# Chunk transposes by DMA, bias in rows, a fixed sync queue and a new order of copies, in a fused attention and MLP kernel

## The chip, the cores and the metric

The kernel runs on one core of a Trainium2 chip. Times are device microseconds of one execution, as the median of several runs. A profile records one execution (of the kernel before a further one of 171.52 us); its span, from first to last instruction, is about 1.7 us shorter than the time. Engines: PE (matrix multiply), PEld (its weight loads), DVE (vector), ACT (activation functions), POOL, and SP, whose queue issues most DMA transfers. L228 is line 228 of that kernel's source; between the two kernels the lines shift by up to four.

## The reference

The input has 2048 rows of 448 columns in bf16. The rows are normalised, and two branches read them: an attention over a window of 8 keys at distance 2, with 16 heads of 28 columns, and an MLP with 1792 hidden columns. The output is the input plus the product of the branches.

```python
xn = _layernorm(x)
s = attention(xn, wqkv, wo)          # 16 heads, Dh = 28, W = 8, dilation 2
g = _silu(gelu(xn @ w1 + b1) @ w2 + b2)
return x + s * g
```

## The kernel before

The rows are cut into four chunks of 512. Feed-forward 1 of a chunk (hT, 14 tiles in seven pairs, k = 0 to 6) alternates with a phase of attention units: scores S, exponential and mask (E), weighted sum psO and its normalisation. Between the units stand feed-forward 2 (ps_y), v, and the output jobs (ps_s, sg, o_t). The order on PE, ACT, DVE and POOL is the program's own. These parts matter:

```python
psA = ctx.enter_context(tc.tile_pool(name="psA", bufs=2, space=PSUM))   # pairs of ps_h, S
psB = ctx.enter_context(tc.tile_pool(name="psB", bufs=4, space=PSUM))   # all else, and pairs 0 and 3 of ps_h
# ... loads on the sync queue: x chunk 0, wv, wraw, x chunk 1, then
nc.sync.dma_start(b1t[:], B_b1.rearrange("(m f) -> f m", f=P))          # 2-byte elements
# ... w1, w2, b2bc, x chunk 2, x chunk 3, 16 pieces of wo

def feed_forward_1(c, ps, wos):
    nc.scalar.preload_act_table_set(SET_GELU)
    for k in range(0, MT // 2, 2):
        ...                                    # pairs k and k+1 with their gelu
        if k == 2 and c in (1, 2):
            q_job(c + 1, 0); k_job(c + 1, 0, nc.vector.tensor_copy)
        if k in (2, 4) and c == 0:             # chunk 1 transposed on PE
            for j in (k - 2, k - 1):
                ln_put(nx + j, ln_tr(nx + j), nc.vector.tensor_copy)
        if c and k in (2, 4 if c == 3 else 6): # tanh on ACT, g on DVE
            ...                                # two silu_job
        for _ in range(2):
            if k >= (2 if c == 3 else 4) and wos:
                wo_job(wos.pop(0))
    nc.scalar.preload_act_table_set(SET_EXP)
    if c + 2 < NC:
        ln_rstd(nx + 4, 4)

# first unit of a phase: scores, exponentials and masks, then q and k of groups 2 and 3,
# then psO
```

The softmax here doesn't subtract the row's maximum and nothing guards it: scores larger than these inputs give would overflow.

Of the kernel before, what the change touches and what calls it, by code (L numbers as in the profile page):

```python
# [9 lines left out]
BF16 = mybir.dt.bfloat16  # L10
# [6 lines left out]
P = 128  # L17
# [16 lines left out]
def kernel(  # L34
# [46 lines left out]
    lnv = const.tile([P, NT], F32, name="lnv")  # L81
    ident = const.tile([P, P], BF16, name="ident")
    eps_t = const.tile([P, 1], F32, name="eps_t")
    b1t = const.tile([P, MT], BF16, name="b1t")
    b1f = const.tile([P, MT], F32, name="b1f")
    b2bc = const.tile([P, D], BF16, name="b2bc")
    mk_gen = const.tile([P, QW], BF16, name="mk_gen")
# [14 lines left out]
    for dst, c0, c1 in ((wv, 2 * D, 3 * D), (wraw, 0, 2 * D)):  # L102
        nc.sync.dma_start(dst[:, 0:3, 0:c1 - c0], A_wqkv[0:384, c0:c1].rearrange("(k p) f -> p k f", p=P))
        nc.sync.dma_start(dst[:64, 3, 0:c1 - c0], A_wqkv[384:448, c0:c1])
    nc.sync.dma_start(x_sb[1][:, :, :], dram_rows(x_par, 4, 4))
    nc.sync.dma_start(b1t[:], B_b1.rearrange("(m f) -> f m", f=P))
    for c0, c1 in ((0, F // 2), (F // 2, F)):
        nc.sync.dma_start(w1[:, 0:3, c0:c1], B_w1[0:384, c0:c1].rearrange("(k p) f -> p k f", p=P))  # L108
        for r in (0, 64):
            nc.sync.dma_start(w1[r:r + 64, 3, c0:c1], B_w1[384:448, c0:c1])  # L110
    nc.sync.dma_start(w2[:, :, :], B_w2.rearrange("(m p) c -> p m c", p=P))
    nc.sync.dma_start(b2bc[:], B_b2.rearrange("(o d) -> o d", o=1).to_broadcast((P, D)))  # L112
    nc.sync.dma_start(x_sb[2][:, :, :], dram_rows(x_par, 8, 4))
    nc.sync.dma_start(x_sb[3][:, :, :], dram_rows(x_par, 12, 4))


    nc.gpsimd.memset(ident[:], 0.0)
# [11 lines left out]
    for tl in (qT, kT):  # L129
        nc.vector.memset(tl[:, :, 0:LEAD].bitcast(U32), 0)  # L130
        nc.vector.memset(tl[:, :, LEAD + S:LQ].bitcast(U32), 0)
    for g in range(4):
        for h in range(4):
            r = (4 * g + h) * DH
            nc.sync.dma_start(wo[32 * h + 1:32 * h + 1 + DH, g, :], A_wo[r:r + DH, :])

    def late_constants():

        nc.vector.memset(mk_gen[:], 1.0)
        nc.gpsimd.affine_select(out=mk_gen[:], in_=mk_gen[:], compare_op=ALU.is_ge, fill=0.0,  # L140
                                base=0, pattern=[[-1, QW]], channel_multiplier=1)
        nc.gpsimd.affine_select(out=mk_gen[:], in_=mk_gen[:], compare_op=ALU.is_ge, fill=0.0,
                                base=7, pattern=[[1, QW]], channel_multiplier=-1)

        nc.gpsimd.affine_select(out=mk_0[:], in_=mk_gen[:], compare_op=ALU.is_ge, fill=0.0,
                                base=-7, pattern=[[0, QW]], channel_multiplier=1)

        q_odd = S // 2 - 8 * QB
        nc.gpsimd.affine_select(out=mk_8[:], in_=mk_gen[:], compare_op=ALU.is_ge, fill=0.0,
                                base=-(q_odd + 7), pattern=[[0, QW]], channel_multiplier=1)  # L150
        nc.gpsimd.tensor_copy(mk_8[:, 0:q_odd], mk_gen[:, 0:q_odd])
        nc.gpsimd.tensor_copy(b1f[:], b1t[:])


    def ln_stats(t):
# [17 lines left out]
            nc.tensor.transpose(pT[:, kt, :], xnb[t % 4][:, kt * P:(kt + 1) * P], ident[:])  # L173
        return pT

    def ln_put(t, pT, copy=None):
        (copy or nc.scalar.copy)(xnT[:, :, LEAD + t * P:LEAD + (t + 1) * P], pT[:, :, :])  # L177

    def ln_dma(t):
        nc.sync.dma_start_transpose(xnT[:, :, LEAD + t * P:LEAD + (t + 1) * P], xnb[t % 4][:, :])  # L180
# [123 lines left out]
        return put  # L304


    def wo_mm(t):
        ps = psB.tile([P, D], F32, name="ps_s", tag="B")
        for g in range(4):
            nc.tensor.matmul(ps[:, :], oT[:, g, t * P:(t + 1) * P], wo[:, g, :],  # L310
                             start=(g == 0), stop=(g == 3))
        return ps

    def wo_put(t, ps, cs=slice(0, D)):
        sg = work.tile([P, D], BF16, name="sg", tag="sg", bufs=3)
        nc.vector.scalar_tensor_tensor(out=sg[:, cs], in0=ps[:, cs], scalar=0.5, in1=g_sb[t % NG][:, cs],  # L316
                                       op0=ALU.mult, op1=ALU.mult)
        o_t = work.tile([P, D], BF16, name="o_t", tag="o_t", bufs=3)
        nc.vector.tensor_tensor(out=o_t[:, cs], in0=xt(t)[:, cs], in1=sg[:, cs], op=ALU.add)
        nc.sync.dma_start(dram_rows(out_par, t, 1)[:, 0, cs], o_t[:, cs])  # L320
# [2 lines left out]
        wo_put(t, wo_mm(t))  # L323


    def qk_unit(b, between=lambda: None):

        E = work.tile([P, 4, 4, P], BF16, name="E", tag="E", bufs=2)
        Sp = [psA.tile([P, 2, 4, P], F32, name="S", tag="A") for _ in range(2)]
        o = LEAD + QB * b  # L330
        for g in range(4):
            for h in range(4):
                r = slice(32 * h, 32 * h + DH)
                nc.tensor.matmul(Sp[h // 2][:, h % 2, g, 0:QW], kT[r, g, o - 7:o - 7 + P],  # L334
                                 qT[r, g, o:o + QW], start=True, stop=True)
        mk = {0: mk_0, 8: mk_8}.get(b, mk_gen)
        for p2 in range(2):
            ev = E[:, 2 * p2:2 * p2 + 2, :, 0:QW]
            nc.scalar.activation(ev, Sp[p2][:, :, :, 0:QW], ACT.Exp, scale=SCALE)  # L339
            mkb = mk[:, :].unsqueeze(1).unsqueeze(1).to_broadcast((P, 2, 4, QW))  # L340
            nc.vector.tensor_tensor(out=ev, in0=ev, in1=mkb, op=ALU.mult)  # L341
            if p2 == 0:
                between()
        return E

    def av_unit(b, E):
# [24 lines left out]
    def feed_forward_1(c, ps, wos):  # L371

        nc.scalar.preload_act_table_set(SET_GELU)
        nx = 4 * (c + 1)
        gelu(0, ps)
        for k in range(0, MT // 2, 2):
            if k:
                ps = ffn1_even(c, k)
                gelu(k, ps)
            if k + 1 < MT // 2:  # L380
                ps = ffn1_odd(c, k + 1)
                gelu(k + 1, ps)
            if c + 2 < NC and k < 4:
                ln_stats(nx + 4 + k)
                ln_stats(nx + 5 + k)
            if k == 2 and c in (1, 2):
                q_job(c + 1, 0)
                k_job(c + 1, 0, nc.vector.tensor_copy)
            if k in (2, 4) and c == 0:

                for j in (k - 2, k - 1):
                    ln_put(nx + j, ln_tr(nx + j), nc.vector.tensor_copy)
            if c and k in (2, 4 if c == 3 else 6):
                h = 0 if k == 2 else 2
                silu_job(4 * (c - 1) + h)
                silu_job(4 * (c - 1) + h + 1)
            for _ in range(2):
                if k >= (2 if c == 3 else 4) and wos:
                    wo_job(wos.pop(0))
        nc.scalar.preload_act_table_set(SET_EXP)  # L400
        if c + 2 < NC:
            ln_rstd(nx + 4, 4)


    with tc.manual_schedule(engines={ENG.PE, ENG.Activation, ENG.DVE, ENG.Pool}):
        nc.scalar.preload_act_table_set(SET_EXP)
        busy(9)
        ln_stats(0)
# [24 lines left out]
        ln_put(3, pT[3])  # L433
        v_put(2, v2)
        v_job(3)
        for which in range(2):
            for kt in range(KT):
                qk_weights(which, kt)
        y_sb = work.tile([P, 4, D + 4], F32, name="y", tag="stage", bufs=1)
        late_constants()  # L440
        for g in range(4):
            q_job(0, g)
            if g == 3:
                ln_stats(7)
                ln_rstd(4, 4)
            else:
                ln_stats(4 + g)
            k_job(0, g)
        ps = ffn1_even(0, 0)
        for t in range(4, 8):  # L450
            ln_apply(t)

        units = iter(range(NB))
        for c in range(3):
            feed_forward_1(c, ps, [[], [0, 1], [2, 3, 4, 5]][c])
            n = c + 1
            qk = [(q_job, g) if w == 0 else (lambda c, g: k_job(c, g, nc.vector.tensor_copy), g)
                  for g in range(1 if c else 0, 3) for w in range(2)] + [(q_job, 3), (k_job, 3)]
            for f, g in qk[:-4]:
                f(n, g)  # L460
            norm = lambda: None
            vs = iter(range(4 * n, 4 * n + (5 if c == 2 else 4)))
            for i in range(5):
                b = next(units)
                E = qk_unit(b)
                norm()
                if i == 0:
                    for f, g in qk[-4:]:
                        f(n, g)
                else:  # L470
                    ffn2_job(4 * c + i - 1)
                    v_job(next(vs))
                    if n + 1 < NC:
# [23 lines left out]
        silu_job(13)  # L497
        silu_psum(14, y14, slice(0, D))

        halves = (slice(0, D // 2), slice(D // 2, D))  # L500
        y15 = [ffn2_biased(psA, "A", 15, halves[0])]
        wo_put(13, s13)
        s14 = wo_mm(14)
        g = g_sb[15 % NG]
        silu_psum(15, y15[0], halves[0])
        wo_put(14, s14)
        y15.append(ffn2_biased(psA, "A", 15, halves[1]))
        s15 = wo_mm(15)
        silu_psum(15, y15[1], halves[1])
        for cs in halves:  # L510
            wo_put(15, s15, cs)
# [1 line left out]
_INS = ['A_x', 'A_wqkv', 'A_wo', 'B_x', 'B_w1', 'B_b1', 'B_w2', 'B_b2']  # L513
_OUTS = [((1, 2048, 448), 'bfloat16')]
# [25 lines left out]
```

## Time and profile before

| | before |
|---|---|
| median time | 171.23 us (171.17 to 171.34, 4 runs) |
| span of the profile | 169.8 us |
| PE / ACT / DVE busy | 161.6 / 124.6 / 116.2 us |
| PE idle before psO, phases of chunks 1, 2, 3 | 0 / 1.46 / 0.46 us |
| load rate from 9.5 to 12.5 us | 60 GB/s |

PE is the bound, so the reading goes by its starts. The ends of matmuls in the profile are modelled and overlap the next start; a time from start to start is safe. A line of the timeline has start, duration, engine, source line, operation, output and inputs, shapes, count, and in brackets the idle time before it with what ended it.

These are lines of the timeline of the kernel before:

```profile
9.06 1.98 PE L207 MATMUL ps_v<-wv,xnT 128*128 128x448 bf16 x8
10.88 1.46 PE L192 MATMUL ps_qk<-xnT,wqk 128*128 128x512 bf16 x6
...
9.47 0.59 ACT L177 COPY xnT<-pT 128x512 bf16<-128x512 bf16 x1
```

The eight v matmuls are merged into one line though they are two groups: the second four need the copy that ends at 10.06. They start at 10.12 and take 0.76 us, so q follows at 10.88 with no wait.

### The profile page before, as it was taken

Reading aid. Unit: us, or ns where it says so; the run is one execution under the profiler, and the core shown is the slowest. Engines: PE = TensorE matmul, PEld = TensorE weight load, DVE = VectorE, ACT = ScalarE, POOL = GpSimd, SP = SyncE. Lnnn points to the kernel's source line nnn. Section 1 sums busy time; section 2 is a strip of 40 time slices with the busy share of each in tenths; the row PEclk is TensorE's granted clock in tenths of the full one; section 3 lists DMA queues with packets and bytes.
Section 4 is the critical chain, followed back from the end, with each engine's and each line's share of the span. In section 5 each row is a group of like instructions: output and inputs, shape, how many; then the busy total and the mean of one; then the engine's idle time right before and its main releaser. Section 6 shows DMA issues by size and latency. Waiting matters only on the chain.

```text
span 169.8 us, 3258 instructions
## 1 busy us (share of the span) xinstructions
PE 161.6 (95%) x1301; PEld 75.2 (44%) x1312; DVE 116.2 (68%) x262; ACT 124.6 (73%) x195; POOL 4.6 (3%) x17
## 2 busy tenths in 40 slices
PE   6999999999999999979999999998999999999990
PEld 2444344345554344335555434444555434445580
DVE  6968708677888664478888614499777513697883
ACT  3764696748888698586888698585888698798840
POOL 7012000000000000000000000000000000000000
PEclk9999999999999999999999999999999999999999
DMA  4969992100131100100111100110000000120011
GB/s 136 287 106 350 343 334 70 30 2 4 31 35 31 31 0 4 54 0 0 35 31 35 31 0 0 54 53 6 0 4 0 0 4 2 54 81 27 4 56 54
DMA packets 15487, 10.09 MB, mean 59 GB/s; under 512 B 7216, under 2 KB 15472, under 8 KB 15472
## 3 DMA queue, kind: packets, MB, share of 16 engines
q1 hardware_dynamic: 15184, 9.66, 20.3%
q10 hardware_dynamic: 288, 0.23, 0.4%
q8 instruction: 10, 0.16, 0.4%
q14 instruction: 5, 0.04, 0.1%
HBM read 7.00 MB, written 1.84 MB: 52 GB/s over the span
## 4 chain that ended last, share of the span: by engine, by line
PE 70%; DVE 9%; SPq 8%; DMA 5%; ACT 5%; issue 1%
PE ps_y L261 23%; PE ps_h L228 17%; PE ps_qk L192 6%; PE ps_v L207 6%; PE ps_s L310 6%; DMA x<-in_A_x_dram 5%; SPq L108 4%; PE ps_h L237 3%; PE psO L350 3%; PE ps_yb L274 3%; PE S L334 3%; SPq L112 2%; ACT hT L243 1%; SPq L110 1%; DVE st L157 1%
## 5 line engine op out<-in xcount | busy, mean ns | idle before, releaser
L243 ACT ACTIVATE hT<-ps_h,b1f 128x512 bf16<-128x512 f32 x56 | 34.1, 694 | 8.9 <-PE ps_h L237 7.5
L228 PE MATMUL ps_h<-xnT,w 128*128 128x512 bf16 x161 | 39.8, 380 | 0.5 <-issue 0.2
L261 PE MATMUL ps_y<-w,hT 128*128 128x448 bf16 x196 | 39.5, 353 | 0.0
L339 ACT ACTIVATE E<-S 128x976 bf16<-128x976 f32 x34 | 31.6, 982 | 5.2 <-PE S L334 4.1
L192 PE MATMUL ps_qk<-xnT,wqk 128*128 128x512 bf16 x124 | 29.1, 379 | 0.5 <-DVE xnT L177 0.3
L261 PEld LDWEIGHTS <-hT 128*128 128x128 bf16 x196 | 18.0, 98 | 16.7
L228 PEld LDWEIGHTS <-w 128*128 128x128 bf16 x168 | 15.2, 98 | 21.1 <-issue 5.1
L341 DVE TENSOR_TENSOR E<-E,mk_gen 128x976 bf16<-128x976 bf16 x30 | 19.9, 666 | 5.2 <-ACT E L339 5.1
L192 PEld LDWEIGHTS <-wqk 128*128 128x128 bf16 x128 | 12.2, 97 | 15.1 <-issue 1.2
L359 DVE TENSOR_TENSOR oT<-psO,den 128x484 bf16<-128x484 f32 (+1 forms) x17 | 11.2, 661 | 10.1 <-ACT den L358 10.1
L291 DVE SCALAR_TENSOR_TENSOR g<-th,y 128x448 bf16<-128x448 bf16 x13 | 7.6, 622 | 12.9 <-ACT th L290 12.9
L207 PE MATMUL ps_v<-wv,xnT 128*128 128x448 bf16 x68 | 15.7, 353 | 0.1
L195 DVE CAST qT<-ps_qk 128x512 bf16<-128x512 f32 x16 | 10.9, 682 | 7.1 <-PE ps_qk L192 7.1
L212 ACT CAST vw<-ps_v 128x448 bf16<-128x448 f32 x17 | 9.0, 532 | 6.8 <-PE ps_v L207 6.8
L310 PE MATMUL ps_s<-wo,oT 128*128 128x448 bf16 x64 | 13.6, 353 | 0.0
L357 ACT ACTIVATE den<-den 128x484 f32<-128x484 f32 (+1 forms) x17 | 10.3, 605 | 4.0 <-DVE den L354 4.0
L157 DVE BATCH_NORM_STATS2 st<-x 128x6 f32<-128x448 bf16 x16 | 9.7, 609 | 4.9 <-DMA x<-in_A_x_dram 4.7
L316 DVE SCALAR_TENSOR_TENSOR sg<-ps_s,g 128x448 bf16<-128x448 f32 (+1 forms) x17 | 10.1, 592 | 3.6 <-PE ps_s L310 3.6
L354 DVE STREAM_SHUFFLE den<-psO 128x484 f32<-128x484 f32 (+1 forms) x17 | 11.7, 695 | 0.0
L358 ACT ACTIVATE den<-den 128x484 f32<-128x484 f32 (+1 forms) x17 | 10.3, 605 | 0.5
L195 ACT CAST kT<-ps_qk 128x512 bf16<-128x512 f32 x7 | 4.1, 582 | 7.1 <-PE ps_qk L192 7.1
L207 PEld LDWEIGHTS <-xnT 128*128 128x128 bf16 x68 | 6.3, 98 | 6.0 <-ACT xnT L177 0.6
(67 smaller groups left out, 138.8 us busy)
## 6 DMA issues: line engine op xcount, KB each, us to landing
out_dram<-o_t SPq DMA_DIRECT2D x15, 112.0 KB
w<-in_B_w_dram SPq DMA_DIRECT2D x1, 1568.0 KB
x<-in_A_x_dram SPq DMA_DIRECT2D x3, 448.0 KB
w<-in_B_w_dram SPq DMA_DIRECT2D x2, 672.0 KB
wraw<-in_A_wqkv_dram SPq DMA_DIRECT2D x1, 672.0 KB
w<-in_B_w_dram SPq DMA_DIRECT2D x4, 112.0 KB
wo<-in_A_wo_dram SPq DMA_DIRECT2D x16, 24.5 KB
wv<-in_A_wqkv_dram SPq DMA_DIRECT2D x1, 336.0 KB
```

The source lines that it names most:

```text
L157: nc.vector.bn_stats(out=st[:], in_=xt(t))
L192: nc.tensor.matmul(ps[:, :], wqk[:, kt, 16 * which + 4 * g:16 * which + 4 * g + 4, :], xnT[:, kt, LEAD + c * CH:LEAD + (c + 1) * CH], star ...
L195: copy((qT, kT)[which][:, g, LEAD + c * CH:LEAD + (c + 1) * CH], ps[:, :])
L207: nc.tensor.matmul(ps[:, :], xnT[:, kt, o:o + P], wv[:, kt, :], start=(kt == 0), stop=(kt == KT - 1))
L228: nc.tensor.matmul(ps[i][:, :], w1[:, kt, m * P:(m + 1) * P], xnT[:, kt, LEAD + c * CH:LEAD + (c + 1) * CH], start=(first and kt == 0), st ...
L243: nc.scalar.activation(hT[:, m, :], ps[i][:, :], ACT.Gelu_apprx_tanh, bias=b1f[:, m:m + 1])
L261: nc.tensor.matmul(ps[:, :], hT[:, m, tt * P:(tt + 1) * P], w2[:, m, :], start=(m == 0), stop=(m == MT - 1))
L310: nc.tensor.matmul(ps[:, :], oT[:, g, t * P:(t + 1) * P], wo[:, g, :], start=(g == 0), stop=(g == 3))
L339: nc.scalar.activation(ev, Sp[p2][:, :, :, 0:QW], ACT.Exp, scale=SCALE)
L341: nc.vector.tensor_tensor(out=ev, in0=ev, in1=mkb, op=ALU.mult)
L354: nc.vector.stream_shuffle(den[:, :, 0:n], psO[:, :, 0:n], [0] * 32)
L359: nc.vector.tensor_tensor(out=oT[:, :, QB * b:QB * b + n], in0=psO[:, :, 0:n], in1=den[:, :, 0:n], op=ALU.mult)
```

## The change

Its intent: take the transposes of chunk 1 off PE, give the loads an order in which nothing needed early stands behind something slow, and keep ACT and DVE from holding up the first attention unit of each phase. The order of the sync queue (ENG.SP) is now fixed to the program's own, too, so that the late loads stay behind the transposes. The diff, cut to its core:

```diff
+    nc.sync.dma_start(b1r[:], B_b1.rearrange("(m f) -> m f", f=P))
     nc.sync.dma_start(x_sb[1][:, :, :], dram_rows(x_par, 4, 4))
-    nc.sync.dma_start(b1t[:], B_b1.rearrange("(m f) -> f m", f=P))
     # ... w1
+    nc.sync.dma_start(x_sb[2][:, :, :], dram_rows(x_par, 8, 4))
     nc.sync.dma_start(w2[:, :, :], B_w2.rearrange("(m p) c -> p m c", p=P))
     # b2bc, x chunk 3 and wo go to late_loads()
@@ feed_forward_1
-            if k == 2 and c in (1, 2):
+            if c + 1 < NC and k == (4 if c == 0 else 2):
                 q_job(c + 1, 0)
                 k_job(c + 1, 0, nc.vector.tensor_copy)
-            if k in (2, 4) and c == 0:
-                for j in (k - 2, k - 1):
-                    ln_put(nx + j, ln_tr(nx + j), nc.vector.tensor_copy)
-            if c and k in (2, 4 if c == 3 else 6):
-                # two silu_job
-            for _ in range(2):
+            for _ in range(4 if c == 2 else 2):
                 if k >= (2 if c == 3 else 4) and wos:
                     wo_job(wos.pop(0))
+            if c and k in (2, 4):
+                silu_job(4 * (c - 1) + k - 2)
+                silu_job(4 * (c - 1) + k - 1)
         nc.scalar.preload_act_table_set(SET_EXP)
-        if c + 2 < NC:
-            ln_rstd(nx + 4, 4)
@@ main
-    with tc.manual_schedule(engines={ENG.PE, ENG.Activation, ENG.DVE, ENG.Pool}):
+    with tc.manual_schedule(engines={ENG.PE, ENG.Activation, ENG.DVE, ENG.Pool, ENG.SP}):
+        pb = psB.tile([P, MT], BF16, name="pb", tag="B")       # after the last v_job
+        nc.tensor.transpose(pb[:, :], b1r[:, :], ident[0:MT, 0:MT])
+        nc.vector.tensor_copy(b1f[:], pb[:, :])
         for t in range(4, 8):
             ln_apply(t)
+            ln_dma(t)
+        late_loads()
@@ first unit of a phase
-                E = qk_unit(b)
-                norm()
-                    for f, g in qk[-4:]:                       # q2, k2, q3, k3
-                        f(n, g)
+                    E = qk_unit(b, lambda: q_job(n, 2))        # q2 between scores and masks
+                    if n + 1 < NC:
+                        ln_rstd(4 * n + 4, 4)
+                    k_job(n, 2)                                # cast on ACT
+                    q_job(n, 3)
+                    k_job(n, 3)
@@ tail: the last tile
-        halves = (slice(0, D // 2), slice(D // 2, D))
+        pieces = (slice(0, 336), slice(336, D))                # ps_s in pieces too
```

More of the change, by code (lines that the diff above doesn't have):

```diff
@@ L83 @@
     eps_t = const.tile([P, 1], F32, name="eps_t")
-    b1t = const.tile([P, MT], BF16, name="b1t")
+    b1r = const.tile([MT, P], BF16, name="b1r")
     b1f = const.tile([P, MT], F32, name="b1f")
@@ L110 @@
             nc.sync.dma_start(w1[r:r + 64, 3, c0:c1], B_w1[384:448, c0:c1])
+    nc.sync.dma_start(x_sb[2][:, :, :], dram_rows(x_par, 8, 4))
     nc.sync.dma_start(w2[:, :, :], B_w2.rearrange("(m p) c -> p m c", p=P))
-    nc.sync.dma_start(b2bc[:], B_b2.rearrange("(o d) -> o d", o=1).to_broadcast((P, D)))
-    nc.sync.dma_start(x_sb[2][:, :, :], dram_rows(x_par, 8, 4))
-    nc.sync.dma_start(x_sb[3][:, :, :], dram_rows(x_par, 12, 4))
     nc.gpsimd.memset(ident[:], 0.0)
@@ L131, with late_loads @@
         nc.vector.memset(tl[:, :, LEAD + S:LQ].bitcast(U32), 0)
-    for g in range(4):
-        for h in range(4):
-            r = (4 * g + h) * DH
-            nc.sync.dma_start(wo[32 * h + 1:32 * h + 1 + DH, g, :], A_wo[r:r + DH, :])
+    def late_loads():
+        nc.sync.dma_start(b2bc[:], B_b2.rearrange("(o d) -> o d", o=1).to_broadcast((P, D)))
+        nc.sync.dma_start(x_sb[3][:, :, :], dram_rows(x_par, 12, 4))
+        for g in range(4):
+            for h in range(4):
+                r = (4 * g + h) * DH
+                nc.sync.dma_start(wo[32 * h + 1:32 * h + 1 + DH, g, :], A_wo[r:r + DH, :])
     def late_constants():
@@ L151, in late_constants @@
         nc.gpsimd.tensor_copy(mk_8[:, 0:q_odd], mk_gen[:, 0:q_odd])
-        nc.gpsimd.tensor_copy(b1f[:], b1t[:])
     def ln_stats(t):
@@ L174, in ln_tr, with ln_put @@
         return pT
-    def ln_put(t, pT, copy=None):
-        (copy or nc.scalar.copy)(xnT[:, :, LEAD + t * P:LEAD + (t + 1) * P], pT[:, :, :])
+    def ln_put(t, pT):
+        nc.scalar.copy(xnT[:, :, LEAD + t * P:LEAD + (t + 1) * P], pT[:, :, :])
     def ln_dma(t):
@@ L304, in silu_exp_job, with wo_mm @@
         return put
-    def wo_mm(t):
+    def wo_mm(t, cs=slice(0, D)):
+        n = cs.stop - cs.start
         ps = psB.tile([P, D], F32, name="ps_s", tag="B")
         for g in range(4):
-            nc.tensor.matmul(ps[:, :], oT[:, g, t * P:(t + 1) * P], wo[:, g, :],
+            nc.tensor.matmul(ps[:, 0:n], oT[:, g, t * P:(t + 1) * P], wo[:, g, cs],
                              start=(g == 0), stop=(g == 3))
@@ L315, in wo_put @@
         sg = work.tile([P, D], BF16, name="sg", tag="sg", bufs=3)
-        nc.vector.scalar_tensor_tensor(out=sg[:, cs], in0=ps[:, cs], scalar=0.5, in1=g_sb[t % NG][:, cs],
+        nc.vector.scalar_tensor_tensor(out=sg[:, cs], in0=ps[:, 0:cs.stop - cs.start], scalar=0.5, in1=g_sb[t % NG][:, cs],
                                        op0=ALU.mult, op1=ALU.mult)
@@ L323, in wo_job, with qk_unit @@
         wo_put(t, wo_mm(t))
-    def qk_unit(b, between=lambda: None):
+    def qk_unit(b, after_scores=lambda: None):
         E = work.tile([P, 4, 4, P], BF16, name="E", tag="E", bufs=2)
@@ L335, in qk_unit @@
                                  qT[r, g, o:o + QW], start=True, stop=True)
+        after_scores()
         mk = {0: mk_0, 8: mk_8}.get(b, mk_gen)
@@ L341, in qk_unit @@
             nc.vector.tensor_tensor(out=ev, in0=ev, in1=mkb, op=ALU.mult)
-            if p2 == 0:
-                between()
         return E
@@ L385, in feed_forward_1 @@
                 ln_stats(nx + 5 + k)
-            if k == 2 and c in (1, 2):
+            if c + 1 < NC and k == (4 if c == 0 else 2):
                 q_job(c + 1, 0)
                 k_job(c + 1, 0, nc.vector.tensor_copy)
-            if k in (2, 4) and c == 0:
-                for j in (k - 2, k - 1):
-                    ln_put(nx + j, ln_tr(nx + j), nc.vector.tensor_copy)
-            if c and k in (2, 4 if c == 3 else 6):
-                h = 0 if k == 2 else 2
-                silu_job(4 * (c - 1) + h)
-                silu_job(4 * (c - 1) + h + 1)
-            for _ in range(2):
+            for _ in range(4 if c == 2 else 2):
                 if k >= (2 if c == 3 else 4) and wos:
                     wo_job(wos.pop(0))
+            if c and k in (2, 4):
+                silu_job(4 * (c - 1) + k - 2)
+                silu_job(4 * (c - 1) + k - 1)
         nc.scalar.preload_act_table_set(SET_EXP)
-        if c + 2 < NC:
-            ln_rstd(nx + 4, 4)
-    with tc.manual_schedule(engines={ENG.PE, ENG.Activation, ENG.DVE, ENG.Pool}):
+    with tc.manual_schedule(engines={ENG.PE, ENG.Activation, ENG.DVE, ENG.Pool, ENG.SP}):
         nc.scalar.preload_act_table_set(SET_EXP)
@@ L456 @@
             n = c + 1
-            qk = [(q_job, g) if w == 0 else (lambda c, g: k_job(c, g, nc.vector.tensor_copy), g)
-                  for g in range(1 if c else 0, 3) for w in range(2)] + [(q_job, 3), (k_job, 3)]
-            for f, g in qk[:-4]:
-                f(n, g)
+            q_job(n, 1)
+            k_job(n, 1, nc.vector.tensor_copy)
             norm = lambda: None
@@ L464 @@
                 b = next(units)
-                E = qk_unit(b)
-                norm()
                 if i == 0:
-                    for f, g in qk[-4:]:
-                        f(n, g)
-                else:
+                    E = qk_unit(b, lambda: q_job(n, 2))
[4 more added lines that the diff above has]
+                    k_job(n, 3)
+                else:
+                    E = qk_unit(b)
+                    norm()
                     ffn2_job(4 * c + i - 1)
@@ L498 @@
         silu_psum(14, y14, slice(0, D))
-        halves = (slice(0, D // 2), slice(D // 2, D))
-        y15 = [ffn2_biased(psA, "A", 15, halves[0])]
+        pieces = (slice(0, 336), slice(336, D))
+        y15 = ffn2_biased(psA, "A", 15, pieces[0])
         wo_put(13, s13)
         s14 = wo_mm(14)
-        g = g_sb[15 % NG]
-        silu_psum(15, y15[0], halves[0])
+        silu_psum(15, y15, pieces[0])
         wo_put(14, s14)
-        y15.append(ffn2_biased(psA, "A", 15, halves[1]))
-        s15 = wo_mm(15)
-        silu_psum(15, y15[1], halves[1])
-        for cs in halves:
-            wo_put(15, s15, cs)
+        s15 = wo_mm(15, pieces[0])
+        y15 = ffn2_biased(psA, "A", 15, pieces[1])
+        wo_put(15, s15, pieces[0])
+        s15 = wo_mm(15, pieces[1])
+        silu_psum(15, y15, pieces[1])
+        wo_put(15, s15, pieces[1])
 _INS = ['A_x', 'A_wqkv', 'A_wo', 'B_x', 'B_w1', 'B_b1', 'B_w2', 'B_b2']
```

## The prediction

> **What bounds the kernel now.** I read the page first, then the chain that ended last in order of time, then the timeline of each place where that chain leaves the PE, then the table of waits and, for the loads, stretches of DMA activity. The page says what the bound is:
>
> ```profile
> PE 161.6 (95%) x1301; PEld 75.2 (44%) x1312; DVE 116.2 (68%) x262; ACT 124.6 (73%) x195; POOL 4.6 (3%) x17
> PEclk9999999999999999999999999999999999999999
> PE 70%; DVE 9%; SPq 8%; DMA 5%; ACT 5%; issue 1%
> ```
>
> PE is busy 95% of the span of 169.8 us at full clock. A change pays only where it takes PE work out, or where PE stands still. In the steady units (four per chunk, such as 79 to 93 us) the chain is PE alone, and nothing there can be won. It leaves PE in four places: the start, the first attention unit after each feed-forward stage, and the tail. The middle one is plainest in chunk 2's phase, by the chain:
>
> ```profile
> 69.31 0.34 PE ps_h L237 x2
> 69.67 1.27 ACT hT L243 x2
> 70.94 0.93 ACT th L290 x2
> 71.88 1.28 ACT L400
> ...
> 73.71 1.75 ACT E L339 x2
> 75.49 0.67 DVE E L341
> 76.16 0.61 DVE qT L195
> 76.77 0.04 issue
> 76.81 0.40 PE psO L350 x16
> ```
>
> The columns are start, duration, what. Two tanh (L290) sit on ACT ahead of the table load, so the two exponentials start 1 us late, the masks on DVE follow them, and the cast of q comes behind the masks. psO is the seventh tile after q's first one in a pool of four buffers, so it needs that cast, though it does not read it. The timeline shows what PE lost:
>
> ```profile
> 71.72 3.63 PE L192 MATMUL ps_qk<-xnT,wqk 128*128 128x512 bf16 x15
> 76.81 0.40 PE L350 MATMUL psO<-E,vw 128*32 128x122 bf16 x16 [1.46 <-DVE qT L195]
> 112.15 3.82 PE L192 MATMUL ps_qk<-xnT,wqk 128*128 128x512 bf16 x15
> 116.44 0.40 PE L350 MATMUL psO<-E,vw 128*32 128x122 bf16 x16 [0.46 <-DVE qT L195]
> ```
>
> The first chunk's phase has no such loss: there the sixteen projections start at 34.34 and psO at 37.90, 3.56 us for the same work. That is my yardstick. What the first stage pays is other: PE transposes of chunk 1.
>
> ```profile
> 24.26 0.61 PE L173 MATMUL pT<-ident,xnb 128*128 128x128 bf16 x8
> 24.70 1.46 PE L228 MATMUL ps_h<-xnT,w 128*128 128x512 bf16 x6
> 30.47 3.61 PE L192 MATMUL ps_qk<-xnT,wqk 128*128 128x512 bf16 x15 [0.30 <-DVE xnT L177]
> ```
>
> Ends of matmuls are modelled, so I count from start to start: 24.26 to 24.70 is 0.44 us for eight transposes, and it happens twice. The 0.30 us wait comes from the copies of the second eight out of PSUM; they stood behind statistics of chunk 2, whose input landed only at 26.07.
>
> **What the Trainium skill says.** "DMA: Bandwidth & Descriptors", Rules for kernel authors, says that a strided last dimension becomes one descriptor per element. The old bias load is such: 14x128 two-byte elements. The trace agrees. In the stretches of DMA activity (start:end, length, five engines, PE clock, DMA share, GB/s) the rate falls to 60 GB/s for 3 us where it was 334 after:
>
> ```profile
> 9.50:12.50 3.00, 2.82 (x14) 1.24 (x14) 2.20 (x10) 1.60 (x4) 0.29 (x1) 1.00 0.50 60
> 12.50:20.00 7.50, 7.50 (x37) 3.10 (x36) 5.91 (x15) 3.10 (x7) 1.18 (x6) 1.00 1.03 334
> 44.75:45.50 0.75, 0.75 (x6) 0.39 (x4) 0.64 (x1) 0.72 (x2) 0.00 (x0) 1.00 0.86 175
> ```
>
> "VectorE: DVE Perf Modes", The three transpose paths, gives 390 ns for one 128x128 transpose on TensorE and 1309 ns by DMA. The trace differs on the first when they are pipelined: 0.44/8 = 0.055 us of PE each. For the DMA form the queue is occupied 1.19 us for one 128x512 tile (median of the eight of chunks 2 and 3), and the last line above shows its data in 0.75 us, starting 1.3 us after the issue at 43.46. "DMA: Bandwidth & Descriptors", Queues, rings and completion order, says each DMA engine consumes its ring's descriptors in order: new transposes stand behind whatever loads the sync queue issued earlier. That order is the main risk below. "ScalarE: Activation LUTs", What ACT_TABLE_LOAD costs, gives 1283 ns for the load; the trace has 1283 (L400), so it agrees. The count of loads does not change.
>
> **The change, part by part.**
>
> 1. Chunk 1 by DMA. PE loses 16 transposes, 2 x 0.44 = 0.88 us, all of it on the path. DVE loses four copies of 0.41 us, beside the path but for the 0.30 us wait, which goes too. Sum 1.18 us.
>
> 2. Bias in rows. The 2-byte scatter goes: 3 us at 60 instead of 334 GB/s is 3 x (1 - 60/334) = 2.5 us of load time. Loads hardly bound the end now, so this is not a gain by itself; it makes room for part 1. PE gets one small transpose of a 14x128 tile, 0.06 to 0.1 us, DVE one small copy, POOL loses one. There may be a small gain: the wqk copies wait for their weights until 10.30, and PE goes from v to q only at 10.88, where the eight v matmuls from 9.06 at 0.19 us would end near 10.57. If the weights land sooner, up to 0.3 us returns; I count +0.1 net of the new transpose.
>
> 3. New order at each first unit. The two late tanh move to where ACT idles: 1.87 us of idle stand before the last gelu at 69.67, and two tanh take 1.04. q of group 2 is cast before the masks, k of groups 2 and 3 on ACT, and the rstd computation after the exponentials. With T the end of feed-forward 1: PE does 8 projections (1.73), scores (0.33), 16 projections (3.56 by the yardstick, with psO's start included), so psO can start at T+5.6. ACT: gelu to T+1.35, table load to T+2.6, exponentials to T+3.55 and T+4.5; masks to T+5.2. The tile psO needs was cast by T+3.7. So psO no longer waits, with 0.4 us to spare. Gain in chunk 2's phase: 76.81 - (71.72 + 3.56) = 1.53 us. In chunk 3's: 116.44 - (112.15 + 3.56) = 0.73 us. Four output jobs now stand together ahead of the last feed-forward pair there; their DVE work, 4 x 1.01 us and two g of 0.6, starting about 105.8, ends near 111.0, when q's first cast becomes due. That is tight but not late.
>
> 4. Chunk 1's first q and k move into the feed-forward, from its end: same PE work, nothing gained or lost, if the data are there.
>
> 5. The tail, 336 and 112 columns in place of 224 and 224. In the old tail DVE is nearly continuous from 162.07 to 167.25. By start-to-start steps of the old trace (dependent 448-wide pair 0.66, 224-wide 0.43), the new string from 163.80 ends at about 167.15, as the last piece has 112 columns: gain 0.1, and a last store of half the size: 0.05. I count 0.15.
>
> 6. Late loads. b2bc, chunk 3 and the sixteen wo pieces go behind the transposes. They end about 37 us by 16 x 0.65 us of issue from 26 (estimate from the old issue times); first uses are near 41, 55 and 66 us. No cost.
>
> Sum: 1.18 + 0.1 + 1.53 + 0.73 + 0.15 = 3.7 us. From it I take 0.1 for the risk of late transposes: 3.6. 171.2 - 3.6 = 167.6 us.
>
> **The rivals.**
>
> *Transposes late.* They are issued once DVE has normalised the tiles, 19.6 to 21.3 us, and are read by q near 24.26 + 1.39 + 0.54 + 1.31 = 27.5 us. The ring holds w2 ahead of them. In the old trace w2's completion let the queue go on at 24.4; minus 2.5 for the bias, plus 1.4 for chunk 2's input which now precedes it (448 KB at about 334 GB/s), is 23.3 at worst. Issue: four times 1.19 from 19.6 ends at 24.4. Last data: 23.2 + 1.3 + 0.75 = 25.3 by issue, or 23.3 + 4 x 0.75 = 26.3 behind w2. A margin of 1.2 to 2 us; speaks for no wait. If the queue is held by back-pressure, as the first w1 issue was (5.64 us), PE loses up to 1 us: 168.6.
>
> *A new wait in place of the old.* ACT takes casts of k in groups 2 and 3; ps_y needs the buffer of the first of them about 0.6 us after it is free. In chunk 3's phase DVE has no slack around 111. If the margins of 0.4 are overdrawn, half of parts 1 to 3 comes back: 168.5 to 169.
>
> *Only the DMA matters or nothing does.* If PE's losses were only modelled ends, the change would give just the 0.9 of removed work, 170.3. Against it: start-to-start times count real delay, and the chain itself leaves PE there for 7 us.
>
> *More.* If the weights land early (0.3) and the tail gains 0.4, 167.0.
>
> **Range and chances.** Predicted 167.6, range 166.9 to 168.6: down by the fourth rival, up by one late wait. The 2% line is 171.18 x 0.98 = 167.76, just above my number, so faster is only a little likelier than within 2%: 0.56 to 0.43. Slower would take a wrong idea of two parts: 0.01.
>
> **What would show it.** No transposes of chunk 1 on PE and no wait of psO for a q cast at the first unit of chunks 2 and 3 phases; those starts earlier by 2.8 (76.81 to about 74.0) and 3.5 us (116.44 to about 112.9). PE idle before the q projection near 27.5 us below 0.2. The stretch 9.5 to 12.5 us near 330 GB/s. A last DVE end near 163.6. I am wrong if PE waits for a DMA at the moved q, if psO waits for masks instead, or if ps_s or q buffers stall for DVE in chunk 3's phase.

## The result, and the profile after

The time is 168.16 us (168.02 to 168.36, 4 runs) against 171.23, a gain of 3.07 us where 3.6 was forecast; it lies in the range, and the measured class is "within 2%". The ratio is 0.9821 with an interval of 0.9804 to 0.9838.

The page of the changed kernel, its engines and its chain by engine:

```profile
PE 160.6 (96%) x1290; PEld 73.8 (44%) x1301; DVE 113.9 (68%) x256; ACT 126.0 (76%) x198; POOL 4.5 (3%) x16
...
PE 88%; DVE 4%; ACT 2%; DMA 2%; issue 1%; DVEq 0%
```

PE now has 88% of the chain instead of 70%: most of the loads of the start, the copies and the masks have left it. At the first units the timeline shows no bracket before psO any more:

```profile
70.96 3.63 PE L193 MATMUL ps_qk<-xnT,wqk 128*128 128x512 bf16 x15
74.52 0.40 PE L351 MATMUL psO<-E,vw 128*32 128x122 bf16 x16
...
109.86 3.63 PE L193 MATMUL ps_qk<-xnT,wqk 128*128 128x512 bf16 x15
113.42 0.40 PE L351 MATMUL psO<-E,vw 128*32 128x122 bf16 x16
```

Both steps are 3.56 us, the yardstick of the prediction. The reason stands on ACT and DVE in the same window: only the gelu stands ahead of the table load, and q of group 2 is cast ahead of the masks.

```profile
68.91 1.27 ACT L244 ACTIVATE hT<-ps_h,b1f 128x512 bf16<-128x512 f32 x2 [0.94 <-PE ps_h L238]
70.19 1.28 ACT L396 ACT_TABLE_LOAD   x1
71.49 1.86 ACT L342 ACTIVATE E<-S 128x976 bf16<-128x976 f32 x2
72.03 0.69 DVE L196 CAST qT<-ps_qk 128x512 bf16<-128x512 f32 x1 [0.61 <-PE ps_qk L193]
72.64 1.41 DVE L344 TENSOR_TENSOR E<-E,mk_gen 128x976 bf16<-128x976 bf16 x2
```

Where the 3.0 us between the starts of psO come from, read at milestones:

| start of | before | after | gain so far |
|---|---|---|---|
| first statistics (DVE) | 3.40 | 3.67 | -0.27 |
| first q projection | 10.88 | 11.36 | -0.48 |
| psO, phase of chunk 1 | 37.90 | 37.14 | 0.76 |
| psO, phase of chunk 2 | 76.81 | 74.52 | 2.29 |
| psO, phase of chunk 3 | 116.44 | 113.42 | 3.02 |
| end of last DVE instruction | 167.25 | 164.21 | 3.04 |

The two steps of chunks 2 and 3 are 1.53 and 0.73 us, to the hundredth what was worked out. The loss is all at the start, and the tail gave nothing. The start of the changed kernel:

```profile
3.67 0.63 DVE L158 BATCH_NORM_STATS2 st<-x 128x6 f32<-128x448 bf16 x1 [0.40 <-DMA x<-in_A_x_dram]
...
11.25 0.18 PE L431 MATMUL pb<-ident,b1r 14*128 14x14 bf16 x1
11.36 7.08 PE L193 MATMUL ps_qk<-xnT,wqk 128*128 128x512 bf16 x31
27.98 1.89 PE L193 MATMUL ps_qk<-xnT,wqk 128*128 128x512 bf16 x8
```

Two things happened. The first input landed 0.27 us later in this execution. And from the statistics to the first q projection it takes 7.69 us instead of 7.48, which is the small transpose pb on PE. The moved q (chunk 1's first q projection, now inside feed-forward 1) starts at 27.98 and shows no wait, so the transposes came in time.

The stretches of DMA activity (start:end, length, busy time of PE, PEld, DVE, ACT and POOL, PE clock, DMA share, GB/s) show that the slow gap of the scatter is gone, but also something unexpected:

```profile
9.50:12.50 3.00, 2.96 (x14) 1.18 (x16) 2.08 (x11) 1.90 (x4) 0.93 (x4) 1.00 1.08 320
12.50:20.00 7.50, 7.45 (x37) 3.20 (x36) 5.91 (x13) 2.63 (x6) 0.41 (x2) 1.00 1.08 266
```

In this execution the rate was 266 GB/s afterwards, where the kernel before had 334, with the DMA engines as busy. So the loads did not end 2.5 us sooner.

### The profile page after: what moved, and what is told of

Same layout as the page of the kernel before. It is cut to its first block, busy times and chain, and to the rows that moved or that the text cites. A ratio compares the mean times of both kernels' runs of the same rounds, so it can differ in the third digit from the quotient of the medians.

```text
span 166.7 us, 3241 instructions
## 1 busy us (share of the span) xinstructions
PE 160.6 (96%) x1290; PEld 73.8 (44%) x1301; DVE 113.9 (68%) x256; ACT 126.0 (76%) x198; POOL 4.5 (3%) x16
## 4 chain that ended last, share of the span: by engine, by line
PE 88%; DVE 4%; ACT 2%; DMA 2%; issue 1%; DVEq 0%
PE ps_y L262 23%; PE ps_h L229 22%; PE ps_qk L193 17%; PE ps_v L208 8%; PE ps_s L312 6%; PE ps_h L238 5%; PE S L336 3%; PE psO L351 3%; DMA x<-in_A_x_dram 2%; DVE sg L318 1%; PE pT L174 1%; ACT L495 1%; ACT den L359 1%; DVE st L158 1%; ACT den L358 1%
## 5 line engine op out<-in xcount | busy, mean ns | idle before, releaser
L360 DVE TENSOR_TENSOR oT<-psO,den 128x484 bf16<-128x484 f32 (+1 forms) x17 | 11.2, 662 | 10.1 <-ACT den L359 10.1
L318 DVE SCALAR_TENSOR_TENSOR sg<-ps_s,g 128x448 bf16<-128x448 f32 (+2 forms) x17 | 10.1, 594 | 10.7 <-PE ps_s L312 10.6
L312 PE MATMUL ps_s<-wo,oT 128*128 128x448 bf16 (+2 forms) x68 | 13.4, 342 | 0.0
L196 ACT CAST kT<-ps_qk 128x512 bf16<-128x512 f32 x10 | 5.8, 580 | 5.3 <-PE ps_qk L193 5.3
L312 PEld LDWEIGHTS <-oT 128*128 128x128 bf16 x68 | 6.4, 98 | 5.9 <-issue 0.2
```

What stands on the lines that cost most here:

```text
L196: copy((qT, kT)[which][:, g, LEAD + c * CH:LEAD + (c + 1) * CH], ps[:, :])
L312: nc.tensor.matmul(ps[:, 0:n], oT[:, g, t * P:(t + 1) * P], wo[:, g, cs], start=(g == 0), stop=(g == 3))
L318: nc.vector.scalar_tensor_tensor(out=sg[:, cs], in0=ps[:, 0:cs.stop - cs.start], scalar=0.5, in1=g_sb[t % NG][:, cs], op0=ALU.mult, op1=AL ...
```

## The experiments

All runs computed the right output. Each was compared with the kernel before on the same chip; that kernel took 171.18 to 171.23 us in the three groups of runs. Edits are against the changed kernel, whose 168.16 us come from other rounds; only the second run of experiment 1 and the runs of experiment 5 have it in their own rounds. Not every part was undone by itself: the fixed sync queue, the place of the rstd computation and that of the output jobs were not.

### 1. The bias scattered again

```diff
-    nc.sync.dma_start(b1r[:], B_b1.rearrange("(m f) -> m f", f=P))
     nc.sync.dma_start(x_sb[1][:, :, :], dram_rows(x_par, 4, 4))
+    nc.sync.dma_start(b1t[:], B_b1.rearrange("(m f) -> f m", f=P))
-        pb = psB.tile(...); nc.tensor.transpose(pb, b1r, ident[0:MT, 0:MT])
-        nc.vector.tensor_copy(b1f[:], pb[:, :])
+        nc.gpsimd.tensor_copy(b1f[:], b1t[:])
```

> The changed kernel with the bias loaded in two-byte elements again, behind chunk 1's input, and no PE transpose of it. Two effects oppose. Theory (my own after reading the trace of the changed kernel): the small transpose cost 0.20 us on PE, because the step from the last v matmuls to the first q projection grew from 0.77 to 0.97 us; so 0.2 us comes back there. But the chunk 1 transposes stood only about 0.7 us clear of their reader (last data near 27.1, q at 27.98), so a scatter that delays the loads by up to 2.5 us makes PE wait 1 to 2 us at the moved q: about 169.0 to 169.8. Rival: the load rate was lower in the changed kernel anyway (266 in place of 334 GB/s from 12.5 to 20 us) and the scatter's idle time is partly given back, then no wait appears and the time is 168.0.

Measured: 167.87 us (4 runs, 167.86 to 167.97). The theory's late transposes did not come; the rival's time did. Undoing this part of the change makes the kernel faster. Because a fifth of a microsecond is near the spread between groups of runs, the same kernel ran once more in the same rounds as the unedited one:

> The changed kernel with the two-byte bias load, again, now in the same rounds as the unedited one. Theory: 0.2 us faster than the unedited kernel, its PE having no bias transpose between v and q, and equal within 0.1 to the one with the early bias. Rival: the 0.29 us seen before was a difference between chips: equal to the unedited kernel within 0.1.

Measured: 167.92 us (4 runs) against 168.09 of the unedited kernel, 0.17 us faster. From the first statistics at 3.41 to the first q at 10.89 it takes 7.48 us, as in the kernel before. So the bias in rows costs 0.2 us: the transpose stands on PE, which is the bound, and the load time it frees was not needed. Nor did much of it arrive: in the first run with the scatter the queue needed 6.04 us for the four transposes, from 19.95 us, in the second 6.26 us, and in the changed kernel 6.04 us as well, from 20.35.

The traces of the two runs also show that the scatter was blamed for too much. Their pages count about 1780 packets more than that of the changed kernel, about one for each of the 14 x 128 elements, but in the stretch from 9.5 to 12.5 us they still load at 220 and 207 GB/s, against 320 without the scatter and 60 in the kernel before. By these rates the scatter alone costs about 1 us of load time (an estimate: 3 x (1 - 220/320) = 0.9), not 2.5. What else slowed the kernel before stays open.

### 2. Chunk 1 transposed by PE again

```diff
             ln_apply(t)
-            ln_dma(t)
...
+            if c == 0 and k in (0, 2):
+                for j in (k, k + 1):
+                    ln_put(nx + j, ln_tr(nx + j), nc.vector.tensor_copy)
```

> The changed kernel with chunk 1 transposed by PE again, at pairs 0 and 2 of the feed-forward, and everything else kept. Theory: 16 transposes at 0.055 us start to start cost PE 0.9 us, all on the path, and no DVE wait as chunk 2's input now lands early: 169.1 (168.8 to 169.3). Rival: transposes only fill time in which PE would wait for weights or buffers: within 0.3 us of 168.2.

Measured: 169.09 us (4 runs), 0.93 more than the changed kernel. From first q to moved q it takes 28.61 - 11.10 = 17.51 us, against 27.98 - 11.36 = 16.62: 0.89 us for the sixteen transposes, as the theory says. The q projection has no wait for copies here, though PE does the transposes again: the 0.30 us wait went with the earlier load of chunk 2's input, the earlier place of the transposes or both, not with the DMA form. The DMA form is free for PE as long as it lands in time.

### 3. The late tanh, the late casts, and both

```diff
# late tanh
-            if c and k in (2, 4):
+            if c and k in (2, 4 if c == 3 else 6):
# late casts
-                    E = qk_unit(b, lambda: q_job(n, 2))
+                    E = qk_unit(b)
                     if n + 1 < NC:
                         ln_rstd(4 * n + 4, 4)
-                    k_job(n, 2)
+                    q_job(n, 2)
+                    k_job(n, 2, nc.vector.tensor_copy)
```

> The changed kernel with the second pair of tanh back behind the last gelu of chunks 1 and 2's feed-forward, all else kept. Theory: the exponentials start 1.04 us later, the masks end about T+6.2 instead of T+5.2, psO waits for the masks some 0.6 us in two phases: 169.4 (168.9 to 169.7), and the wait named is DVE E, not a q cast. Rival: the new order of the casts alone removed the wait, so the tanh are free: 168.2.

> The changed kernel with q and k of group 2 cast on DVE behind both masks again, all else kept (early tanh, rstd after the exponentials). Theory: q of group 2 is cast about 0.65 us after the masks, near T+5.8 where PE could start psO at T+5.6: a wait of 0.2 to 0.5 us for a q cast in all three phases, 169.0 (168.6 to 169.7). Rival: the early tanh alone removed the wait, so the order of casts is free: 168.2.

Measured: late tanh 169.22 us (4 runs), late casts 168.64 us (4 runs). Both rivals fall: neither half of part 3 did the work alone. With the late tanh psO starts with two matmuls and then stops for a mask; from the start of the sixteen projections at 70.74 the yardstick gives 74.30, so PE loses 0.51 us, and as much in the next phase:

```profile
70.74 3.63 PE L193 MATMUL ps_qk<-xnT,wqk 128*128 128x512 bf16 x16
74.29 0.23 PE L351 MATMUL psO<-E,vw 128*32 128x122 bf16 x2
74.81 0.39 PE L351 MATMUL psO<-E,vw 128*32 128x122 bf16 x14 [0.28 <-DVE E L344]
```

With the late casts psO is 0.18 us late in each of three phases (in the first: 37.06 against 33.32 + 3.56 = 36.88), 0.54 us in sum. Then both were put back.

> The changed kernel with both the second pair of tanh and the group 2 casts back where they were (rstd stays behind the exponentials, output jobs stay in their new places). Alone, the late tanh cost 1.06 us and the late casts 0.48 us by the medians. Theory (one chain in series: tanh, table load, exponential, mask, cast, psO): undone together they cost more than their sum, as the 0.4 us of slack that hides part of each is spent once: psO near T+6.85 where PE could start at T+5.6, about 1.2 us in each of two phases and 0.18 in the first, 170.6 (170.2 to 170.9), with psO waiting for a q cast. Rival (independent waits): the costs add to 1.5 us, 169.7.

Measured: 170.49 us (4 runs), 2.33 more than the changed kernel, where the single costs add to 1.54. The series theory holds:

```profile
70.85 3.63 PE L193 MATMUL ps_qk<-xnT,wqk 128*128 128x512 bf16 x15
75.52 0.40 PE L351 MATMUL psO<-E,vw 128*32 128x122 bf16 x16 [1.04 <-DVE qT L196]
```

psO is 1.11 us late here and again in chunk 3's phase, and waits for a cast of q, as in the kernel before. Tanh, table load, exponential, mask, cast are one chain, and the slack at its end is there once.

Two moves of part 3 that no run undoes can be read by comparing this run with the kernel before. In chunk 2's phase the kernel before lost 1.53 us and this run 1.11; up to that psO the rstd computation is the only part of the old order that this run does not restore. In the kernel before its two activations (0.30 and 0.21 us) stand on ACT between the table load and the exponentials, in this run behind them, so the missing 0.42 us are put down to them. In chunk 3's phase the kernel before had no rstd computation, and another hold-up: the exponentials were done at 114.11, but the masks started on DVE only at 114.55, behind two output jobs and two casts that fill it from 111.43. The moved output jobs removed that. They also let PE come to its projections earlier against ACT, so that this run, with the output jobs moved, loses more there (1.11 us) than the kernel before (0.73).

### 4. The bias in rows, but off the path

```diff
-    nc.sync.dma_start(b1r[:], B_b1.rearrange("(m f) -> m f", f=P))
+    nc.scalar.dma_start(b1r[:], B_b1.rearrange("(m f) -> m f", f=P))   # third on ACT's queue
         busy(2)
+        pb = psA.tile([P, MT], BF16, name="pb", tag="A")
+        nc.tensor.transpose(pb[:, :], b1r[:, :], ident[0:MT, 0:MT])
```

> The changed kernel with the bias still in rows, but loaded third on the ACT queue behind two pieces of input and transposed on PE beside the warm-up matmuls near 6 us, where PE waits for the first normalised tiles. Theory: the 0.21 us that the transpose costs between v and q is off the path there, so the time is that of the scattered bias, 167.9 (167.8 to 168.1). Rival: the scattered load was faster for another reason (its slow packets free DMA engines for what matters), then this one gains nothing: 168.2. A third outcome: the bias lands later than 6.5 us or the third issue delays ACT's first Ln, then the whole start shifts and it is slower than 168.3.

Measured: 168.00 us (4 runs, 167.80 to 168.05), in the theory's range. Statistics at 3.49, first q at 10.98: 7.49 us, the 0.2 us is back. The transpose now runs at 6.21 us, where PE waits for normalised rows.

### 5. The second weights behind the transposes, and the unedited kernel beside it

```diff
-    nc.sync.dma_start(w2[:, :, :], B_w2.rearrange("(m p) c -> p m c", p=P))
     def late_loads():
+        nc.sync.dma_start(w2[:, :, :], B_w2.rearrange("(m p) c -> p m c", p=P))
# and the edit of experiment 4
```

> The changed kernel once more, unedited, as the yardstick of these rounds: 168.1 to 168.3. Its trace also tells whether the first statistics at 3.67 us in the profile on record (3.39 to 3.54 in the other traces) were chance: I expect 3.4 to 3.5 here, and the step from those statistics to the first q projection unchanged at 7.69 us.

> The changed kernel with the bias transposed beside the warm-up, and the second weights loaded behind the four transposes instead of ahead of them. Theory: PE never waited for the transposes (margin 0.7 to 1 us), so only the bias counts: 0.2 us faster than the unedited kernel of these rounds, and the transposes' last data near 25 instead of 27 us. Rival: the margin was overdrawn in some runs, then it is 0.3 us or more faster; or the second weights now come late for their first use near 37 us, then it is slower.

Measured: 168.09 us (5 runs) for the unedited kernel and 167.84 us (4 runs) for this one: 0.25 us, close to what the bias alone is worth. From first q to moved q it takes 16.61 us in both, so PE waited for the transposes in neither. The second weights do delay them: with these behind, the four issues take 5.24 us, each 1.20 to 1.31; in the run of experiment 4, the same but for the place of these weights, one of the four takes 1.95, and in the changed kernel 2.01. Landing near 25 us was too hopeful, though: the last issue starts at 23.84, which by the estimate of the next experiment is ready at 26.4. This version has the lowest median, though its runs overlap with those of the scatter (167.89 to 168.04), and the step from the changed kernel is small.

The unedited kernel's first statistics stood at 3.62 us, and again 7.69 us passed to the first q; so the expectation of 3.4 to 3.5 missed. The late first input was seen in both profiles of the unedited kernel and not in variants that share its first loads (3.38 to 3.54). Its timed runs spread from 168.02 to 168.36, which this would fit. I take it for chance, but no run settles it.

### 6. All loads ahead of the transposes

```diff
+        late_loads()
         for t in range(4, 8):
             ln_apply(t)
             ln_dma(t)
-        late_loads()
```

> The changed kernel with the late loads (b2, chunk 3's input, sixteen pieces of wo) issued before the four transposes of chunk 1, in the fixed order of the sync queue. Theory: the queue is in order, and the sixteen small issues alone take 8 to 11 us of it; from about 19 us that puts the first transpose near 30 and the last data near 35, so PE waits 6 to 8 us at the moved q (27.8 us in the changed kernel): 174 to 177. Rival: the issues before 19 us, which nothing holds up, take most of it: a wait under 2 us, 168.5 to 170.

Measured: 179.32 us, one look, state unknown. The theory's mechanism is right and its time too short. These are PE lines of its timeline:

```profile
36.19 3.57 PE L193 MATMUL ps_qk<-xnT,wqk 128*128 128x512 bf16 x8 [8.31 <-DMA xnT<-xnb]
...
42.38 1.90 PE L193 MATMUL ps_qk<-xnT,wqk 128*128 128x512 bf16 x8
```

The first bracket is the wait that the prediction's rival "Transposes late" feared: 8.31 us. But the same eight matmuls take 3.57 us at 36.19 and 1.90 at 42.38. The stretches explain it (the column after POOL's is the granted PE clock):

```profile
28.00:36.00 8.00, 0.00 (x0) 0.00 (x0) 0.00 (x0) 1.19 (x2) 0.00 (x0) 0.72 0.40 84
...
40.00:42.00 2.00, 2.00 (x6) 0.57 (x4) 0.49 (x1) 0.00 (x0) 0.00 (x0) 0.55 0.00 0
42.00:44.00 2.00, 2.00 (x11) 0.79 (x10) 0.55 (x1) 1.50 (x3) 0.00 (x0) 1.00 0.00 0
```

PE stood still for 8 us. Its clock was granted at 1.00 up to 31.5 us, 3.6 us after the modelled end of the last matmul at 27.88; at 0.50 in the stretches from 32 to 40, at a mean of 0.55 from 40 to 42, which is full speed for the last tenth, and at 1.00 after. By start to start, from moved q (36.19) to scores (44.21) it takes 8.02 us; at full clock, in the late-casts run, it took 32.99 - 27.72 = 5.27. So 2.75 us of the 11.2 are the clock, the rest the wait. The Trainium skill, "TensorE: Matmul & The Clock Gate", What's actually happening, describes this: the clock passes half of its pulses after an idle window of about 3.4 us. This run agrees with the half rate and, by its 3.6 us, with the window.

The run also dates the landing. Its chain ends the wait so:

```profile
33.61 2.45 DMA xnT<-xnb
...
36.19 3.57 PE ps_qk L193 x8
```

From the issue of the last transpose to its reader there are 2.6 us. In the changed kernel the four issues take from 20.35 to 26.39, and the last starts at 25.18. My estimate from these: it is ready at 25.18 + 2.6 = 27.8 us, and its reader starts at 27.98. The margin is 0.2 us, not the 1.2 to 2 of the prediction. In the second run with the scatter the same sum gives 24.92 + 2.6 = 27.5 us for a reader that starts at 27.50 and does not wait either, so the estimate is good to about 0.1 us, and the margin is close to nothing.

### 7. The tail

```diff
# halves again
-        pieces = (slice(0, 336), slice(336, D))
+        pieces = (slice(0, D // 2), slice(D // 2, D))
# another run: residual adds of tiles 13 and 14 on POOL
-        wo_put(13, s13)
+        wo_put(13, s13, add=nc.gpsimd.tensor_tensor)
-        wo_put(14, s14)
+        wo_put(14, s14, add=nc.gpsimd.tensor_tensor)
```

> The changed kernel with the last tile in halves of 224 columns again. Theory (DVE sets the tail, its work is the same in sum): within 0.1 us of the changed kernel, 168.1 to 168.3. Rival (the size of the last piece sets the end, as my prediction counted 0.15 us): 168.3 to 168.4.

> The changed kernel with the residual adds of tiles 13 and 14 on POOL instead of DVE. In the tail DVE runs without a gap worth naming from 159.05 to 164.21 us (5.16 us; 5.18 in the kernel before). Theory: DVE sets the end, two adds of 0.39 us leave it, and the end comes 0.3 to 0.5 us sooner, then bound by the last tanh (162.98): 167.7 to 167.9. Rival: the last PE piece and its tanh set the end, or POOL shares something with DVE that slows it: 168.1 to 168.6.

Measured: halves 168.11 us (4 runs), adds on POOL 168.28 us (4 runs). The split of the last tile is worth nothing. The last tanh ends at 162.98 in the changed kernel and its g starts only at 163.31, so a third of a microsecond of DVE work is ahead of it; but taking two adds away did not give it back:

```profile
161.00 0.51 DVE L283 SCALAR_TENSOR_TENSOR g<-th,ps_yb 128x336 bf16<-128x336 bf16 x1 [0.40 <-ACT th L282]
162.12 1.03 POOL L321 TENSOR_TENSOR o_t<-x,sg 128x448 bf16<-128x448 bf16 x1 [0.40 <-DVE sg L318]
162.49 0.85 DVE L321 TENSOR_TENSOR o_t<-x,sg 128x336 bf16<-128x336 bf16 x1
```

The first add's place is filled by 0.40 us of waiting for the tanh of the 336 columns. The second add runs beside DVE's own add, which takes 0.85 us here and 0.33 in the changed kernel: it ends at 163.34, just after POOL's at 163.15. "SBUF — State Buffer", Who interferes with whom, says that a DVE instruction with two SBUF inputs contends with a POOL instruction that reads SBUF, and the second to start is blocked. This trace agrees that DVE is held up, by 0.5 us. So the theory that the end simply follows DVE's work falls: of the two adds taken away one was replaced by a wait for a tanh, the other by a collision. What a tail without the collision would gain was not tried.

## Why the prediction was right, and where its steps failed

The time lies in the range and the bound, the mechanism and most terms hold; the gain was 0.5 us smaller than forecast. Of the classes the prediction gave "faster" 0.56 and "within 2%" 0.43; it came out as the second.

**Part 1, 1.18 us: right.** The sixteen transposes cost 0.89 us by experiment 2, and in the trace of the changed kernel the 0.30 us wait is gone. But the same experiment shows no such wait with PE transposes, so the prediction put these 0.30 us down to the wrong edit: the new places of loads and transposes took it away.

**Part 2, "+0.1 net of the new transpose": wrong in sign.** It measured -0.2 us (7.69 against 7.48 us from statistics to q, and two runs with the scatter). The step that failed is "the eight v matmuls from 9.06 at 0.19 us would end near 10.57": they are two groups, and the second waits for a copy until 10.06, so q was never held by its weights. The second run with the scatter confirms it: there the weight copies started at 8.75 instead of 10.30, and the step from statistics to q stayed at 7.48. The 0.06 to 0.1 us for the transpose was also short: the gap between v and q grew by 0.2. The sentence "Loads hardly bound the end now" was right, and should have led to the conclusion that this part can only cost.

**Part 3, 1.53 and 0.73 us: right to the hundredth.** The sizes had to come out once the wait was gone, as they are measured against the same work without it; what could have failed was the slack. It was worked out as 0.4 us and was enough: in chunk 2's phase the masks end at 74.05 and psO starts at 74.52. Experiment 3 shows that it takes both moves, and that the rstd computation and the output jobs had a share.

**Part 4: right.** No gain, no loss.

**Part 5, 0.15 us: not there.** The step that failed is "as the last piece has 112 columns: gain 0.1": DVE's string from the first g to the end is 5.16 us after and 5.18 before, and halves run as fast.

**Part 6: right,** with nothing waiting for the late loads: no PE line after 28 us has a wait.

**The rivals.** Late transposes did not happen, but that was in part luck, as their margin was badly estimated. Three terms were short: the first issue came at 20.35 us, not 19.6; the last one started 4.83 us later, not 3 x 1.19 = 3.57, as one issue was held up behind the second weights; and from there to the reader it took 2.6 us, not 1.3 + 0.75. The step "minus 2.5 for the bias" failed as well: the load rate was lower afterwards in this run, and with the scatter back the four issues take about as long (6.04 and 6.26 us). What the lower rate comes from stays open; it was 282 to 313 GB/s in the variants that load the same way, and 319 to 322 with the scatter. The new waits for casts did not come.

In sum the trace has 1.19 + 1.53 + 0.73 = 3.45 us of gains, less 0.21 for pb, less 0.27 for the first input in the profiled run: about 3.0 at psO, and 3.07 by the timed runs. Against the 3.7 us of the prediction's sum, part 2 explains 0.3 and part 5 0.15; the rest, about 0.2 us, is near the 0.27 us of the first input, which is taken for chance.

## What to carry to other kernels

Work out a wait from start to start against a stretch of the same work without the wait; such terms came out exact here where the wait went altogether, while a gain guessed from a merged line had the wrong sign. Where PE is the bound, an instruction added to it costs its whole step however small, unless it stands where PE waits anyway; a slow load that nobody waits for is better left alone. Casts and activations ahead of an exponential form one chain, so shorten all of it, and check how much margin a transfer has before putting loads ahead of it in the same queue.

## What the Trainium skill lacked or had wrong

- "VectorE: DVE Perf Modes", The three transpose paths: its 390 ns for TensorE is not what a transpose costs in a full stream; 16 of them took 0.89 us, 0.056 us each. "TensorE: Matmul & The Clock Gate", Wait — 56ns, not 53.3ns?, has the figure that fits, 55.6 ns from start to start at 128 columns.
- The same table's 1309 ns for the DMA form is for 128x128 and does not say what a transfer holds up: for one 128x512 tile the runs show 2.6 us from issue to reader, and of the queue 1.19 us each when alone and 6.04 us for four behind the second weights.
- "TensorE: Matmul & The Clock Gate", What's actually happening: the way back to full clock is given as at least one window of about 3.4 us of sustained work; the run with the wait worked at 0.50 from 36.2 to about 41.8 us, 5.6 us, so well above that least figure.
- "SBUF — State Buffer", Who interferes with whom: no durations for a POOL add in bf16, and no other page has one; 128x448 took 1.03 us on POOL against 0.39 on DVE.
